# The first stage of an attention, Fourier and expert kernel cut into finer steps and put into a new order

## The chip, the cores and the metric

The kernel runs on one core of a Trainium2 chip. The metric is the device time of one execution in microseconds (us). Five engines work side by side, each on its own queue and in its queue's order: PE (matrix products), DVE (vector), ACT (scalar functions and copies), POOL (a second elementwise engine) and SP, which here only issues DMAs. An engine waits for another by a semaphore.

## What is computed

```python
def reference(**kwargs):
    attn_out = _attn_ref(q, k, v, mem_k, mem_v)        # 4 x 8 heads, 768 rows, chunks of 32 rows with 56 + 8 keys
    x = attn_out.transpose(0, 2, 1, 3).reshape(B, S, H * D)
    x = _moe_ref(x, w_ch1, w_ch2)                      # u = x + real(fft2(x)); u + relu(norm(u) @ w_ch1) @ w_ch2
    return _moe2_ref(x, w_in, conv_w, w_out)           # h = relu(x @ w_in); h * sigmoid(conv3(h)) @ w_out
```

Four batches of 768 rows and 512 columns; the inner widths are 2048 and 1024. The dense weights come as 64-bit floats and are taken apart on the chip ("decoded") into a high and a low part.

## The kernel before

**First stage.** Attention is done in 32 units of 96 rows. For one unit: scores (8 products `sc`, written to a pair of PSUM tiles of which there is only one pair), row maxima of each head (`sm`, `ngm` on DVE), exponentials (ACT, in place in `sm`), transposes in two halves (`atp` on PE, copied to `at`), the product with the values (`o`), the division (`r`, `xn` on DVE), sums and differences of mirrored columns (`xf` on POOL) and a second transpose (`xtp`, copied to `xT`). After seven or eight units of a batch its Fourier transform can begin (function `dft`: folds, products `z`, products `p`, centring `pm`, then `uc`, the result). After that comes `dense(b)`, the first quarter of the hidden width for both halves of the batch: four blocks `h` with copies `hh` (ACT) and `hl` (DVE), four blocks `y`, each copied out. All of these products share four rotating PSUM banks, later (from the third part on, pool `ps_g2`) three.

**Decoding.** One weight block of 128x512 passes through seven DVE and ACT operations (lines 124 to 140), spread over four steps `W`; 24 blocks are decoded up to the main loop and in its first turns.

**The order.** A string, `SCHED`, line 38, says in which order steps are recorded; `task` (line 549) plays a letter: S scores and row maxima, E exponentials of half a unit, A transposes of half a unit and their copy, P values product and division, X second transpose and its copy, B one step of the transform, D one step of `dense`, W one step of decoding, F one filler product (`keep`, line 204), H one step of the split of the first chunk of the main loop. Every engine's queue gets its instructions in this order. `ENGINES` says which engine does which copy or sum. A bar in the string divides it into three parts: with the attention, the rest of the transforms, the rest of `dense`. Then follows the main loop (lines 748 to 786): for a chunk and block f a product group `h` (12 products), and two turns later four groups `acc`, which read `hh` and `hl`. The main loop and the last layer after it are PE-bound and take two thirds of the time.

Of the kernel before, what the change touches and what calls it, by code (L numbers as in the profile page):

```python
# [37 lines left out]
SCHED = "FFFSEAEFSAWFWFFFEEPFFFSFFAFFWWAEPAFXSWFEAWESFFEWWPSFFEFFWXXAAEWWPEAFFSEFFFWAPAFFFEAXFEPAAFFFSFFFFFFWEFEXWPAASWXEWEPAXFFSFFBAPEEAXASFEBPSFAEBBFEFFFWBASEBXPXABASFEBWEBPAESFAWBBXBEPAAEESFBBBWBWXPASFBEABBWWBBBBXPEASFWXEAFFBWWPBEBEWASEBBAXEWPXAAFBSFEBBWEPSABBAWBWEXEDDWDWDPSAABEXDPDBBEBBBDABDAXESBBPDBEEBBXBABSDXBABPSEBBADBBABDPABDEBSEAXBBEBBEEPBSBABXBADBDEBBPEXABASDPBDADBDBBSXEXBDABESBPEABEABDBBSPBADFBBFEBXAEESDBBBBPABABBXDEPDBBAAEBXEBBBXBDBPADABDBPXDDXBB|BBBWDWBDWBBDWBDDDBBWWWBBWDDWBBBBWDWBWWDBDBWBWBWWWBWDWBWDDWWBWBBBWBBDBDBWDDBWBB|DDWDDWWDWWWWWDDWWWDWWHDWHDHDWHDWWWDDDWDWWWWWWW"  # L38
ENGINES = {'at': 'aaaaaaaaavavaaaaaaaaaaaaaaaaaaaaaaaaaaaaaaaaaavaaaavaaavaaaaaaaa', 'xt': 'vvvvaaaaaaaaaaaaavaaaaaaaaavaava', 'y': 'aaaaaaaaaaaaaaaaaaaaaaaaaaaaaaaa', 'uh': 'aaaaaaaaaaavavvvvaaavvaaavavaaaaaaaaaaavvv', 'ul': 'vvpvvvvvvvvvvvvpvvvvvvvvvpvvpppppvpvvvpppv', 'fl': 'pvvvvppvppvvppvp', 'f': 'vpvvvpppvpvpvvpv', 'u0': 'vvvvvvvv', 'u1': 'vvvvvvvv'}
# [7 lines left out]
def fourier_mixer_kernel(ctx: ExitStack, tc: tile.TileContext, qk, vw, w1, w2, w_in, w_out, conv_w,  # L47
# [57 lines left out]
    def decode_all(todo, st=None):  # L105

        st, lo_of = st or fetch(todo[0][0]), None
        for i, (_, where, f, spill) in enumerate(todo):
# [3 lines left out]
            while placed(f) is False:  # L112
                if lo_of is not None:
                    lo_of()
                    lo_of = None
                yield
# [51 lines left out]
    def run(gen, n=1):  # L168
        for _ in range(n):
            if next(gen, "end") == "end":  # L170
                return False
        return True
# [30 lines left out]

    def keep(n):

        p = ps_g.tile([128, 512], F32, tag="g", name="idle")
        for _ in range(n):
            mm(p[:, 0:128], onesm, onesm, start=True, stop=True)  # L208

    NUNITS = NB * NU  # L210
    units = {}
    def load_qk(u):
        if u < NUNITS:
            t = ldp.tile([128, QW + KWD], F32, tag="qk", name="qk", bufs=2)
            units[u] = {"qk": t}
            nc.sync.dma_start(out=t, in_=qk[u])

    def load_v(u):
        if u < NUNITS:
            t = ldp.tile([128, VW], F32, tag="vw", name="vw", bufs=3)  # L220
            nc.sync.dma_start(out=t, in_=vw[u])
            units[u]["vw"] = t

    def scores(u):
# [3 lines left out]
        kT = t[:, QW:QW + KWD].rearrange("p (a k) -> p a k", a=4)  # L228
        sc = [ps_sc.tile([128, 4, KW], F32, tag="sc", name="sc") for _ in range(2)]
        sch = {}  # L230
        for a in range(4):
            for g in range(2):
                sch[2 * a + g] = sc[g][:QB, a, :]
                mm(sch[2 * a + g], qT[64 * g:64 * g + 64, a, :], kT[64 * g:64 * g + 64, a, :], start=True, stop=True)  # L234
        blk = u % NU
        kind = 0 if blk == 0 else (2 if blk == NU - 1 else 1)
        sm = smp.tile([QB, NH, KW], F32, tag="sm", name="sm", bufs=3)
        ngm = smp.tile([QB, NH], F32, tag="ngm", name="ngm")
# [4 lines left out]
        d["ex"], d["ngm"] = sm, ngm  # L243
# [7 lines left out]
    def atr(u, half):  # L251
        d = units[u]
        if half == 0:
            d["at"] = smp.tile([128, NH, QB], F32, tag="at", name="at", bufs=1)
        at = ps_g.tile([128, 4, QB], F32, tag="g", name="atp")
        for i in range(4):
            nc.tensor.transpose(at[:, i, :], d["ex"][:, 4 * half + i, :], ident_sb[:QB, :QB])  # L257
        copy("at", d["at"][:, 4 * half:4 * half + 4, :], at)

    def pv(u):  # L260
# [3 lines left out]
        r = smp.tile([QB, NH], F32, tag="r", name="r")  # L264
        o = ps_o.tile([128, 2, 512], F32, tag="o", name="o")
        oh = o[:QB, :, 0:VW // 2].rearrange("p b (h e) -> p b h e", e=HD + 1)
        for h in range(NH):
            mm(oh[:, h // 4, h % 4, :], at_sb[:, h, :], vw[:, h * (HD + 1):(h + 1) * (HD + 1)], start=True, stop=True)  # L268
        r4 = r.rearrange("p (b h o) -> p b h o", b=2, o=1)
        nc.vector.tensor_scalar(out=r4, in0=oh[:, :, :, HD:HD + 1], scalar1=1e-9, scalar2=None, op0=ALU.add)  # L270
        nc.vector.reciprocal(out=r, in_=r)
        xn = smp.tile([QB, DM + 1], F32, tag="xn", name="xn", bufs=1)
        nc.vector.tensor_tensor(
            out=xn[:, 0:DM].rearrange("p (b h e) -> p b h e", b=2, e=HD), in0=oh[:, :, :, 0:HD],
            in1=r4.to_broadcast([QB, 2, 4, HD]), op=ALU.mult)
        xf = smp.tile([QB, 2, 256], F32, tag="xf", name="xf")
# [5 lines left out]
    xTs = {}  # L282

    def xtr(u):
        d = units.pop(u)
        b, blk = divmod(u, NU)
        if blk == 0:
            xTs[b] = xtp.tile([128, 4, S + 1], F32, tag="xT", name="xT")
        xT = xTs[b]
        xf = d["xf"].rearrange("p a (m c) -> p (a m) c", c=128)  # L290
        p = ps_g.tile([128, 4, QB], F32, tag="g", name="xtp")
        for i in range(4):
            nc.tensor.transpose(p[:, i, :], xf[:, i, :], ident_sb[:QB, :QB])  # L293
# [10 lines left out]
    def dft(b):  # L304
# [3 lines left out]
        for sl, rv in ((slice(97, 385), slice(671, 383, -1)), (slice(0, 97), slice(768, 671, -1))):  # L308
# [3 lines left out]
            while NU * b + NU - 1 in units or count["X"] < NU * b + NU:  # L312
# [21 lines left out]
        def zstep(c, m):  # L334
# [5 lines left out]
            z = ps_g.tile([128, 512], F32, tag="g", name="z")  # L340
# [9 lines left out]
            accumulate(z[:sn, 0:nw], seq)  # L350
            zh = dfp.tile([97, 256], F32R, tag=f"zh{c % 2}{m}", name="zh")
# [6 lines left out]
            if c < 2:  # L358
                nc.vector.tensor_tensor(out=zn[:sn, 1], in0=z[:sn, 256:258], in1=zn[:sn, 0].bitcast(F32),
                                        op=ALU.subtract)  # L360
                ZN[c, m] = zn
            Z[c, m] = (zh, zl, sn)
# [21 lines left out]
        zstep(0, 0)  # L384
        yield from fold(2)
        yield
        zstep(0, 1)
        yield from fold(3)
        yield
        zstep(1, 0)  # L390
        yield
        zstep(1, 1)
# [4 lines left out]
        for m in range(2):  # L397
            zc = slice(128 * m, 128 * m + 128)
            p = ps_g.tile([128, 512], F32, tag="g", name="p")
            accumulate(p[:, 0:194], part(0, 194, zc))  # L400
            accumulate(p[:, 256:448], part(1, 192, zc))
            pj = p.rearrange("p (r j) -> p j r", r=2)
# [16 lines left out]
        def center(hf, gs):  # L419
            ss = slice(hf * HALF, hf * HALF + HALF)  # L420
            pm = ps_g.tile([128, 512], F32, tag="g", name="pm")
            mm(pm[:, 0:HALF], onesm, gs, start=True, stop=True)  # L422
            for m in range(2):
                nc.vector.tensor_tensor(out=G[:, m, ss], in0=G[:, m, ss], in1=pm[:, 0:HALF], op=ALU.subtract)
            nc.scalar.copy(gs[0:1, :], pm[0:1, 0:HALF])
            nc.sync.dma_start(out=mud[b][:, ss], in_=gs[0:1, :])

        gs = summed(0)
        for c in (2, 3):
            for m in range(2):  # L430
                zstep(c, m)
                yield
            center(c - 2, gs)
# [3 lines left out]
        for m in range(2):  # L437
            zc = slice(128 * m, 128 * m + 128)
            p = ps_g.tile([128, 512], F32, tag="g", name="p")
            for c, o, n in ((2, 0, 194), (3, 256, 192)):  # L440
# [4 lines left out]
                accumulate(p[:, o:o + n], seq[-1:], start=False)  # L445
            pj = p.rearrange("p (r j) -> p j r", r=2)
# [11 lines left out]
            yield  # L458
        uc = dfp.tile([128, 4, S], F32, tag="Fhl", name="uc")
        for hf in range(2):  # L460
# [5 lines left out]
            yield  # L466
            yield from split_uc(2 * b + hf, uc[:, :, ss])
            if hf:
                bgb.append(dense(b))
# [14 lines left out]
    def g1(c, f):  # L484
        uh, ul = uhl[c]
        need(("1", f))
        p = ps_g.tile([128, 512], F32, tag="g", name="h")
        accumulate(p[:, 0:TC], split3([(w1h[f][:, k * 128:k * 128 + 128], w1l[f][:, k * 128:k * 128 + 128],
                                        uh[:, k], ul[:, k]) for k in range(4)]))
        hh = a1p.tile([128, TC], F32R, tag="hh", name="hh", bufs=NI)  # L490
# [3 lines left out]
                                       op0=ALU.max, op1=ALU.subtract)  # L494
        hhl[c, f] = (hh, hl)

    def dense(b):
        for hf in range(2):
            c = 2 * b + hf
            for f in range(NI):  # L500
                g1(c, f)
                yield
            for t in range(4):
                ts = slice(t * 128, t * 128 + 128)
                need(*[("2", f) for f in range(NI)])
                p = ps_g.tile([128, 512], F32, tag="g", name="y")
                accumulate(p[:, 0:TC], split3([(w2h[f][:, ts], w2l[f][:, ts]) + hhl[c, f] for f in range(NI)]))
                y = a1p.tile([128, TC], F32, tag="y", name="y")
                copy("y", y, p[:, 0:TC])
                nc.sync.dma_start(out=yd[b][:, t, hf * TC:hf * TC + TC], in_=y)  # L510
# [23 lines left out]
    bga, bgb = [], []  # L534

    def step_of(q):
        moved = False
        while q:
            got = next(q[0], "end")
            if got != "end":  # L540
                return moved or got != "wait"
            q.pop(0)
            moved = True
        return moved

    count = dict.fromkeys("SEAPXW", 0)
    todo = {}

    def task(k):
# [5 lines left out]
        if k == "S":  # L555
            scores(n)
            load_qk(n + 2)
            if n == 0:
                load_v(2)
        elif k == "E":  # L560
            expo(n // 2, n % 2)
            if n == 8:
# [3 lines left out]
                nc.gpsimd.dma_start(out=stab_sb, in_=stab)  # L566
        elif k == "A":
            atr(n // 2, n % 2)
        elif k == "P":
            pv(n)  # L570
            load_v(n + 3)
        elif k == "X":
            xtr(n)
            if n % NU == NU - 2:
                bga.append(dft(n // NU))
        elif k == "F":
            keep(1)
        elif k == "B":
            return step_of(bga)
        elif k == "D":  # L580
            return step_of(bgb)
# [4 lines left out]
    with tc.manual_schedule():  # L586
        load_qk(0)
        nc.scalar.dma_start(out=mask_sb, in_=mask)
        load_qk(1)
# [4 lines left out]
        wdec = decode_all([({"1": w1, "2": w2}[k][f], place, (k, f), None) for k in "12" for f in range(NI)],  # L594
# [438 lines left out]
```

## Time and profile before

| | |
|---|---|
| runs | 1018.87 and 1019.71 us, median of three 1019.71 |
| profiled execution, its own time | 1020.89 us |
| its span, first to last instruction | 1018.1 us |
| busy in the span | PE 98%, DVE 67%, ACT 43%, POOL 21% |
| filler products | 63 (126 instructions), all but two of them before 114 us |
| first block `h` | 117.78 us |
| last four groups `y` of `dense` begin | 334.07 us |
| first product of `acc`, the main loop's | 348.63 us |

A busy PE is a PE with an instruction in flight. The first stage is the only long stretch in which PE is less than full and the other engines are close to full; from 150 us on PE has no gap until 740 us.

### The profile page before, as it was taken

What the parts mean: (1) busy time and instruction counts of PE and PEld (TensorE: products, weight loads), DVE (VectorE), ACT (ScalarE), POOL (GpSimd) and SP (SyncE); (2) the same over time, 40 slices, a digit from 0 to 9 for tenths busy, and PEclk for the clock granted to TensorE, in tenths of its full rate; (3) what the DMA queues carried; (4) which work ended last, traced back from release to release, by engine and by line L of the source; (5) the groups of instructions that cost most, each with busy time, mean ns of one, the idle gap of its engine ahead of it and who ended that gap; (6) DMA issues with size and microseconds to landing.
All of it is one profiled execution on the core that took longest, in us unless ns stands there. A gap on an engine that the chain in (4) does not pass through costs nothing.

```text
span 1018.1 us, 16674 instructions
## 1 busy us (share of the span) xinstructions
PE 999.1 (98%) x6430; PEld 957.6 (94%) x6430; DVE 685.8 (67%) x1508; ACT 442.5 (43%) x923; POOL 214.9 (21%) x232
## 2 busy tenths in 40 slices
PE   7899999999999999999999999999999999999997
PEld 6888989999999999999999999999999999999996
DVE  4889956766988775767787775635357566465554
ACT  4687754664444423333333332212245454454442
POOL 1353251422400000102211000202013222222222
PEclk9999999999999999999999999999999999999999
DMA  6864532522437545575788972818543111010101
GB/s 198 264 185 138 182 105 78 164 72 81 129 100 235 179 152 194 187 182 125 174 201 224 199 183 83 148 49 164 159 123 115 52 69 56 1 62 1 62 1 62
DMA packets 63807, 130.86 MB, mean 129 GB/s; under 512 B 4919, under 2 KB 39199, under 8 KB 63503
## 3 DMA queue, kind: packets, MB, share of 16 engines
q1 hardware_dynamic: 51424, 102.35, 30.6%
q0 software_dynamic: 12048, 27.17, 14.9%
q8 instruction: 50, 0.82, 0.3%
q14 instruction: 29, 0.24, 0.1%
q10 hardware_dynamic: 256, 0.28, 0.1%
HBM read 92.28 MB, written 43.79 MB: 134 GB/s over the span
## 4 chain that ended last, share of the span: by engine, by line
PE 90%; DVE 5%; issue 2%; ACT 1%; DMA 1%; POOL 1%; DVEq 0%; POOLq 0%; ACTq 0%
PE acc L66 32%; PE h L66 25%; PE ph L66 12%; PE y L66 6%; PE o L268 3%; PE sc L234 2%; PE p L66 2%; PE z L66 2%; DVE sm L240 2%; PE atp L257 2%; PE idle L208 1%; PE xtp L293 1%; PE pm L422 1%; ACT sm L248 0%; DMA qk<-in_qk 0%
## 5 line engine op out<-in xcount | busy, mean ns | idle before, releaser
L66 PE MATMUL acc<-hh,w 128*128 128x384 f32 x768 | 208.0, 334 | 0.0
L66 PE MATMUL h<-uh,w 128*128 128x384 f32 x768 | 208.0, 334 | 0.0
L492 ACT ACTIVATE hh<-h 128x384 fp32r<-128x384 f32 x128 | 62.5, 490 | 247.2 <-PE h L66 247.1
L493 DVE SCALAR_TENSOR_TENSOR hl<-h,hh 128x384 fp32r<-128x384 f32 x128 | 70.5, 554 | 145.6 <-ACT hh L492 145.1
L66 PEld LDWEIGHTS acc<-hh,w 128*128 128x128 f32 x768 | 139.8, 188 | 0.0
L66 PEld LDWEIGHTS h<-uh,w 128*128 128x128 f32 x768 | 139.8, 188 | 0.0
L66 PE MATMUL ph<-xh,wit 128*128 128x384 f32 x512 | 136.3, 337 | 0.7 <-ACT hrow L823 0.7
L66 PE MATMUL acc<-hl,w 128*128 128x384 f32 x384 | 128.3, 334 | 0.0
L66 PE MATMUL h<-ul,w 128*128 128x384 f32 x384 | 128.3, 334 | 0.0
L66 PE MATMUL acc<-wot,hgh 128*128 128x512 f32 x384 | 119.6, 393 | 0.0
L831 DVE SCALAR_TENSOR_TENSOR cv<-hrow,cw_sb,cv 128x768 f32<-128x768 f32 x64 | 110.1, 1721 | 3.1 <-ACT cv L825 2.0
L843 POOL TENSOR_TENSOR hgl<-cv,hgh 128x768 fp32r<-128x768 f32 x32 | 60.4, 1886 | 194.6 <-ACT hgh L842 179.0
L837 DVE TENSOR_TENSOR cv<-hrow,cv 128x768 f32<-128x768 f32 x32 | 30.7, 959 | 99.2 <-ACT cv L836 99.1
L66 PEld LDWEIGHTS ph<-xh,wit 128*128 128x128 f32 x512 | 93.3, 188 | 2.6 <-ACT hrow L823 1.4
L66 PE MATMUL ph<-xl,wit 128*128 128x384 f32 x256 | 86.1, 336 | 0.0
L66 PEld LDWEIGHTS acc<-wot,hgh 128*128 128x128 f32 x384 | 71.7, 188 | 13.4
L248 ACT ACTIVATE sm<-sm,ngm 96x128 f32<-96x128 f32 x256 | 80.5, 394 | 7.4 <-DVE ngm L240 7.4
L823 ACT ACTIVATE hrow<-ph 128x384 f32<-128x384 f32 x64 | 31.3, 493 | 102.3 <-PE ph L66 101.1
L66 PE MATMUL acc<-wot,hgl 128*128 128x512 f32 x192 | 74.7, 389 | 0.0
L66 PEld LDWEIGHTS acc<-hl,w 128*128 128x128 f32 x384 | 72.1, 188 | 0.0
L66 PEld LDWEIGHTS h<-ul,w 128*128 128x128 f32 x384 | 72.1, 188 | 0.0
L240 DVE CUSTOM_DVE_ANT_0 sm<-sc,mask_sb 96x128 f32<-96x128 f32 x256 | 56.3, 282 | 18.3 <-PE sc L234 14.5
(150 smaller groups left out, 1879.2 us busy)
## 6 DMA issues: line engine op xcount, KB each, us to landing
w<-in_w SPq DMA_DIRECT2D x32, 512.0 KB, 4.1
qk<-in_qk SPq DMA_DIRECT2D x32, 448.0 KB, 3.5
us<-ucd SPq DMA_DIRECT2D x13, 768.0 KB, 7.9
yp<-yd SPq DMA_DIRECT2D x13, 768.0 KB, 8.4
vw<-in_vw SPq DMA_DIRECT2D x32, 260.0 KB, 3.0
ucd<-uc SPq DMA_DIRECT2D x8, 768.0 KB, 4.7
yd<-y SPq DMA_DIRECT2D x32, 192.0 KB, 2.0
ucd<-mud POOLq DMA_DIRECT2D x8, 768.0 KB, 14.4
```

What stands on the lines that cost most here:

```text
L66: mm(o, a, b, start=(start and i == 0), stop=(stop and i == n - 1))
L234: mm(sch[2 * a + g], qT[64 * g:64 * g + 64, a, :], kT[64 * g:64 * g + 64, a, :], start=True, stop=True)
L240: nc.vector.tensor_tensor_reduce(out=sm[:, h, :], in0=sch[h], in1=mask_sb[:, kind, :], op0=ALU.add, op1=ALU.min, scale=-0.125, scalar=3e38 ...
L248: nc.scalar.activation(out=d["ex"][:, h, :], in_=d["ex"][:, h, :], func=AF.Exp, scale=-1.0, bias=d["ngm"][:, h:h + 1])
L257: nc.tensor.transpose(at[:, i, :], d["ex"][:, 4 * half + i, :], ident_sb[:QB, :QB])
L268: mm(oh[:, h // 4, h % 4, :], at_sb[:, h, :], vw[:, h * (HD + 1):(h + 1) * (HD + 1)], start=True, stop=True)
L492: nc.scalar.activation(out=hh, in_=p[:, 0:TC], func=AF.Relu)
L493: nc.vector.scalar_tensor_tensor(out=hl, in0=p[:, 0:TC], scalar=0.0, in1=hh.bitcast(F32), op0=ALU.max, op1=ALU.subtract)
L823: nc.scalar.activation(out=h[:, 1 + hf * TC:1 + hf * TC + TC], in_=p[:, 0:TC], func=AF.Relu)
L831: nc.vector.scalar_tensor_tensor(out=cv, in0=h[:, j:j + S], scalar=cw_sb[:, j, f:f + 1], in1=cv, op0=ALU.mult, op1=ALU.add)
L837: nc.vector.tensor_tensor(out=cv, in0=h[:, 1:S + 1], in1=cv, op=ALU.mult)
L843: nc.gpsimd.tensor_tensor(out=hgl[i], in0=cv, in1=hgh[i].bitcast(F32), op=ALU.subtract)
```

## The change

Steps are cut finer. S keeps the products alone, and T does the row maxima of half a unit; A and X keep the transposes, and a and x do the copies; P is cut into P (product), p (add), r (reciprocal) and n (multiply and the POOL sums); l and v issue the loads of a unit; B and D yield between a product group and the copies that read it. Assertions check that no step is recorded before the last reader of its buffer. The core of the diff:

```diff
@@ scores
-        for h in range(NH):
+    def rowmax(u, half):
...
+        for h in range(4 * half, 4 * half + 4):
             nc.vector.tensor_tensor_reduce(
@@ atr
         for i in range(4):
             nc.tensor.transpose(at[:, i, :], d["ex"][:, 4 * half + i, :], ident_sb[:QB, :QB])
-        copy("at", d["at"][:, 4 * half:4 * half + 4, :], at)
+
+    def atr_out(u, half):
...
+        copy("at", d["at"][:, 4 * half:4 * half + 4, :], at[:, 0:4 * QB].rearrange("p (a q) -> p a q", a=4))
@@ dense
-                g1(c, f)
+                p = g1(c, f)
...
+                yield "half"
+                g1_out(c, f, p)
                 yield
...
                 accumulate(p[:, 0:TC], split3([(w2h[f][:, ts], w2l[f][:, ts]) + hhl[c, f] for f in range(NI)]))
+                yield "half"
                 y = a1p.tile([128, TC], F32, tag="y", name="y")
                 copy("y", y, p[:, 0:TC])
@@ prelude
-        load_v(0)
-        load_v(1)
-        nc.sync.dma_start(out=sgn_sb, in_=sgn)
...
+                nc.gpsimd.dma_start(out=sgn_sb, in_=sgn)
```

The string and the table of engines are new. The string has 5 letters F where 63 stood. The numbers of products of the other kinds are unchanged, and so are the counts of `sc`, `atp`, `o` and `xtp` that stand ahead of the first `z`. Of the copies of `y`, all on ACT before, 18 of 32 go to DVE now; of the 16 sums `uc`, all on DVE before, 5 go to POOL. The letters W are 33, 27 and 26 in the three parts before, 34, 17 and 36 now. The third parts of the two strings (before, change; a D was a whole step before and is half of one now):

```
DDWDDWWDWWWWWDDWWWDWWHDWHDHDWHDWWWDDDWDWWWWWWW
DDDDDDWWWDDDWDDWDDDWWWDHDWWDWWWDHWWWWWWWWDDWWWWWDWDWWWWWWWWW
```

**PE, the start of the program.** Before (`idle` is the filler):

```order
L208 MATMUL idle<-onesm 128x128 x3
L234 MATMUL sc<-qk 96x128 x8
L257 MATMUL atp<-ident_sb,sm 128x96 x4
L208 MATMUL idle<-onesm 128x128
L234 MATMUL sc<-qk 96x128 x8
L257 MATMUL atp<-ident_sb,sm 128x96 x4
L208 MATMUL idle<-onesm 128x128 x4
L268 MATMUL o<-vw,at 96x65 x8
L208 MATMUL idle<-onesm 128x128 x3
L234 MATMUL sc<-qk 96x128 x8
```

Of the change:

```order
L270 MATMUL sc<-qk 96x128 x8
L227 MATMUL idle<-onesm 128x128
L304 MATMUL atp<-ident_sb,sm 128x96 x4
L270 MATMUL sc<-qk 96x128 x8
L304 MATMUL atp<-ident_sb,sm 128x96 x4
L320 MATMUL o<-vw,at 96x65 x8
L270 MATMUL sc<-qk 96x128 x8
L304 MATMUL atp<-ident_sb,sm 128x96 x8
L270 MATMUL sc<-qk 96x128 x8
```

The products stand in much the same order; the fillers between them are gone.

**DVE, from the end of `dense` to the main loop.** In both programs DVE has four `hl` of the last chunk of `dense`, then decoding, then three `hl` of the main loop in a row, which its first `acc` reads. Before, the last of the four and the rows that follow it (17 rows stand between it and the three `hl`; `whb`, one for a weight block, stands among them three times):

```order
L493 SCALAR_TENSOR_TENSOR hl<-h,hh 128x384
L132 SCALAR_TENSOR_TENSOR whb<-w_4624,wsc 128x512
L136 TENSOR_SCALAR wsc<-whb 128x512
L140 SCALAR_TENSOR_TENSOR w_9_4463<-wlb,wsc 128x512
L124 TENSOR_SCALAR wsc<-w_4673 128x512
L125 TENSOR_SCALAR wlb<-w_4673 128x512
L129 SCALAR_TENSOR_TENSOR wlb<-w_4673,wlb 128x512
L132 SCALAR_TENSOR_TENSOR whb<-w_4673,wsc 128x512
L136 TENSOR_SCALAR wsc<-whb 128x512
L140 SCALAR_TENSOR_TENSOR w_9_4464<-wlb,wsc 128x512
```

Of the change, the same `hl` (here the second of a pair) and what follows; 52 rows stand between it and the three `hl`, with `whb` eight times, three copies of `y` and the split `uh`, `ul` of the first chunk:

```order
L582 SCALAR_TENSOR_TENSOR hl<-h,hh 128x384 x2
L137 SCALAR_TENSOR_TENSOR whb<-w_4359,wsc 128x512
L141 TENSOR_SCALAR wsc<-whb 128x512
L145 SCALAR_TENSOR_TENSOR w_6_3736<-wlb,wsc 128x512
L129 TENSOR_SCALAR wsc<-w_4502 128x512
L130 TENSOR_SCALAR wlb<-w_4502 128x512
L166 COPY y<-y 128x384
L134 SCALAR_TENSOR_TENSOR wlb<-w_4502,wlb 128x512
L137 SCALAR_TENSOR_TENSOR whb<-w_4502,wsc 128x512
L141 TENSOR_SCALAR wsc<-whb 128x512
L145 SCALAR_TENSOR_TENSOR w_7_3737<-wlb,wsc 128x512
```

The decoder stands at block 6 there, where it stood at block 9 before; at the three `hl` of the main loop it stands at block 10 in both.

## Rows read from the trace of the kernel before

**Rows 1.** Stretches: length, then busy us (instructions) by engine, PEclk, DMA share, GB/s.

```profile
0.00:117.78 117.78, 106.27 (x1082) 96.02 (x1083) 93.75 (x463) 82.24 (x238) 39.23 (x70) 1.00 0.63 194
80.00:100.00 20.00, 19.04 (x198) 17.76 (x197) 18.36 (x85) 13.73 (x44) 6.64 (x13) 1.00 0.41 125
100.00:117.78 17.78, 17.33 (x188) 16.01 (x189) 17.30 (x74) 15.30 (x43) 4.61 (x8) 1.00 0.57 178
117.78:180.26 62.48, 60.92 (x512) 58.48 (x510) 42.85 (x168) 34.91 (x101) 23.24 (x31) 1.00 0.32 104
180.26:334.07 153.81, 153.81 (x1129) 150.06 (x1129) 123.09 (x312) 76.32 (x185) 40.25 (x49) 1.00 0.40 130
```

**Rows 2.** Timeline of PE, first stage: start, us, what, count [idle before, releaser].

```profile
5.05 2.02 PE L234 MATMUL sc<-qk 64*96 64x128 f32 x16 [2.31 <-DMA qk<-in_qk]
9.60 2.03 PE L234 MATMUL sc<-qk 64*96 64x128 f32 x16
13.76 1.50 PE L268 MATMUL o<-vw,at 128*96 128x65 f32 x16
15.91 1.12 PE L234 MATMUL sc<-qk 64*96 64x128 f32 x16
...
25.50 1.32 PE L234 MATMUL sc<-qk 64*96 64x128 f32 x16 [1.01 <-DVE ngm L240]
...
47.73 1.83 PE L208 MATMUL idle<-onesm 128*128 128x128 f32 x14
49.40 0.49 PE L293 MATMUL xtp<-ident_sb,xf 96*128 96x96 f32 x4
```

**Rows 3.** Timeline of DVE, the first row maximum of the kernel.

```profile
7.10 0.29 DVE L240 CUSTOM_DVE_ANT_0 sm<-sc,mask_sb 96x128 f32<-96x128 f32 x1 [6.05 <-PE sc L234]
```

**Rows 4.** Chain of work that ended last, 100 to 131 us: start, us, what.

```profile
99.90 0.42 PE idle L208 x2
...
110.83 1.74 DVE uc L166 x2
...
123.35 2.43 DVE wlb L129
...
130.10 2.35 PE y L66 x12
```

**Rows 5.** Groups by line, 0 to 300 us: busy us, mean ns | idle before.

```profile
L161 DVE COPY at<-atp 128x384 f32<-128x384 f32 x5 | 2.7, 548 | 0.2 <-PE atp L257 0.2
L166 POOL TENSOR_TENSOR Fhl<-F,Fhl 128x386 fp32r<-128x386 f32 x4 | 4.4, 1100 | 11.8 <-ACT Fhl L325 11.8
```

**Rows 6.** Timeline of PE, end of dense to main loop.

```profile
334.07 0.33 PE L66 MATMUL y<-hh,rxc 128*128 128x384 f32 x1
...
348.63 0.34 PE L66 MATMUL acc<-hh,w 128*128 128x384 f32 x1
348.81 0.34 PE L66 MATMUL acc<-hl,w 128*128 128x384 f32 x1
```

**Rows 7.** Timeline of DVE, the same place.

```profile
321.94 0.69 DVE L140 SCALAR_TENSOR_TENSOR w<-wlb,wsc 128x512 fp32r<-128x512 int32 x1
...
325.25 0.69 DVE L140 SCALAR_TENSOR_TENSOR w<-wlb,wsc 128x512 fp32r<-128x512 int32 x1
...
331.01 1.82 DVE L166 TENSOR_TENSOR ul<-us,uh 128x768 fp32r<-128x768 f32 x2
...
334.80 0.56 DVE L493 SCALAR_TENSOR_TENSOR hl<-h,hh 128x384 fp32r<-128x384 f32 x1 [0.43 <-ACT hh L492]
335.27 0.68 DVE L132 SCALAR_TENSOR_TENSOR whb<-w,wsc 128x512 int32<-128x512 int32 x1
...
341.71 0.69 DVE L132 SCALAR_TENSOR_TENSOR whb<-w,wsc 128x512 int32<-128x512 int32 x1 [3.04 <-ACT wsc L128]
...
347.37 0.43 DVE L124 TENSOR_SCALAR wsc<-w 128x512 int32<-128x512 int32 x1 [0.47 <-DMA w<-in_w]
...
348.05 1.01 DVE L493 SCALAR_TENSOR_TENSOR hl<-h,hh 128x384 fp32r<-128x384 f32 x2
```

More of the change, by code (lines that the diff above doesn't have):

```diff
@@ L166, in either, with run @@
         (nc.vector if vector(what) else nc.gpsimd).tensor_tensor(out=out, in0=in0, in1=in1, op=op)
[L168 to L172, printed above, removed]
+    def run(gen):
+        return next(gen, "end") not in ("end", "wait")
     def rxt(tag, name):
@@ L202, in fourier_mixer_kernel, with bank, taken, after @@
     sgn_sb = cst.tile([128, 1], F32, name="sgn_sb")
+    banks = []
+    def bank(name):
+        i = len(banks) - PSG
+        assert i < 0 or banks[i][1], "the bank's last product is still unread"
+        t = ps_g.tile([128, 512], F32, tag="g", name=name)
+        banks.append([t, False])
+        return t
+    def taken(*tiles):
+        for entry in banks[-PSG:]:
+            entry[1] |= any(entry[0] is t for t in tiles)
+    def after(k, n):
+        assert count[k] >= n, "a step comes before the last reader of its buffer"
     def keep(n):
-        p = ps_g.tile([128, 512], F32, tag="g", name="idle")
+        p = bank("idle")
+        taken(p)
         for _ in range(n):
@@ L211, in fourier_mixer_kernel, with home @@
     units = {}
[L212 to L222 removed]
+    loop = [u for u in range(NUNITS) if u not in AHEAD]
+    def home(u):
+        d = units.setdefault(u, {})
+        if u in AHEAD and "home" not in d:
+            d["home"] = a1p.tile([128, 4 * TC], F32R, tag=AHEAD[u], name="qv").bitcast(F32)
+        return d
+    def load_qk(u):
+        d = home(u)
+        if u in AHEAD:
+            d["qk"] = d["home"][:, 0:QW + KWD]
+        else:
+            if loop.index(u) > 1:
+                after("S", loop[loop.index(u) - 2] + 1)
+            d["qk"] = ldp.tile([128, QW + KWD], F32, tag="qk", name="qk", bufs=2)
+        nc.sync.dma_start(out=d["qk"], in_=qk[u])
+    def load_v(u):
+        d = home(u)
+        if u in AHEAD:
+            d["vw"] = d["home"][:, QW + KWD:QW + KWD + VW]
+        else:
+            if loop.index(u) > 2:
+                after("P", loop[loop.index(u) - 3] + 1)
+            d["vw"] = ldp.tile([128, VW], F32, tag="vw", name="vw", bufs=3)
+        nc.sync.dma_start(out=d["vw"], in_=vw[u])
     def scores(u):
@@ L282, in fourier_mixer_kernel, with xtr_out @@
     xTs = {}
+    spent, spent_u = set(), set()
     def xtr(u):
-        d = units.pop(u)
+        d = units[u]
+        xf = d["xf"].rearrange("p a (m c) -> p (a m) c", c=128)
+        p = d["xtp"] = bank("xtp")
+        p = p[:, 0:4 * QB].rearrange("p (a q) -> p a q", a=4)
+        for i in range(4):
+            nc.tensor.transpose(p[:, i, :], xf[:, i, :], ident_sb[:QB, :QB])
+    def xtr_out(u):
+        xp = units.pop(u)["xtp"]
+        p = xp[:, 0:4 * QB].rearrange("p (a q) -> p a q", a=4)
+        taken(xp)
         b, blk = divmod(u, NU)
         if blk == 0:
+            assert b < 2 or b - 2 in spent, "the rows before last are still read"
             xTs[b] = xtp.tile([128, 4, S + 1], F32, tag="xT", name="xT")
         xT = xTs[b]
[L290 to L293, printed above, removed]
         xo = xT[:, :, blk * QB:(blk + 1) * QB]
@@ L466, in dft @@
             yield
+            assert b == 0 or 2 * b + hf - 2 in spent_u, "the chunk before last is still read"
             yield from split_uc(2 * b + hf, uc[:, :, ss])
             if hf:
-                bgb.append(dense(b))
+                split_done.add(b)
             yield
@@ L533, in fourier_mixer_kernel, with all_dft, all_dense @@
     wit = []
[L534 to L546, printed above, removed]
+    def all_dft():
+        for b in range(NB):
+            while count["x"] < NU * b + NU - 1:
+                yield "wait"
+            yield from dft(b)
+    def all_dense():
+        for b in range(NB):
+            while b not in split_done:
+                yield "wait"
+            yield from dense(b)
+    split_done = set()
+    count = dict.fromkeys("lvSTEAaPprnXxWBDH", 0)
     todo = {}
@@ L630, in fourier_mixer_kernel @@
         ps_g.release()
+        assert all(entry[1] for entry in banks)
+        banks.clear()
         ps_g = tc.alloc_tile_pool(name="ps_g2", bufs=3, space=PSUM, reuse_waits="tile")
```

138 lines of the change are left out of this document (95 added, 43 removed).

## The prediction

> **What bounds the kernel now.** I read the table of stretches first, then PE's own timeline in the first stage, then the chain of work that ended last, and at last the timelines of DVE and PE where `dense` hands over to the main loop. From 180 us on PE is busy without a gap [rows 1], so whatever is won ahead is kept only if PE is fed through the end of `dense` as it is now. The first stage is another matter. Up to the first `h` at 117.78 us PE shows 106.27 us of work, DVE 93.75 and ACT 82.24 [rows 1]. That PE figure is swollen by fillers: 14 instructions, which are 7 fillers, take from 47.73 to 49.40 us, 1.67 us, so one costs 0.24 us [rows 2]; the 61 that stand ahead of the first `h` make 14.6 us. The work that counts on PE is therefore some 91.7 us, less than DVE's. PE also waits for DVE, as for the 1.01 us before the scores at 25.50 [rows 2]. DVE cannot begin on row maxima before 7.10 us [rows 3]; from there to 117.78 it has 110.7 us and fills some 93.5 of them, 84%. Late in the stage it fills more: 18.36 of 20 us (92%) and 17.30 of 17.78 (97%) [rows 1], and the chain there goes mostly through DVE, with few pieces of filler [rows 4]. So the first stage is bound by DVE and by waits among three engines, not by the fillers.
>
> **The change, part by part.**
>
> *Fillers.* 58 go, 58 x 0.24 = 13.9 us of PE. That is no gain by itself where the next product waits for DVE; it is room for PE.
>
> *Finer steps.* They remove no product and add no operation. They let DVE and ACT do other work between a product and its copy. How full DVE then gets sets the first `h`. Its work ahead of that point also shrinks by 6.7 us: counted over the rows ahead of the first `h` in both orders, four `uc` sums are gone (1.74 for two, so 3.5 us [rows 4]; two go to POOL, two stand later), three `xT` copies and one `at` copy go to ACT (4 x 0.5 = 2.0 us by the 548 ns of such a copy [rows 5], less overlap) and two subtractions `Fhl` go to POOL (about 1.2 us together on DVE; 1.1 us each on POOL [rows 5]). POOL has the room, 39.23 of 117.78 us busy [rows 1]; with no cover its slower sums would put some 2 to 3 us on the way to the first `h`. That leaves 93.5 - 6.7 = 86.8 us. With DVE full all the time the first `h` would come at 93.9; PE, 91.7 us of work from 5.05 on [rows 2], cannot be there before 96.8; at 92% of DVE it is 7.1 + 86.8/0.92 = 101.4; at today's 84% it is 110.4. With three engines this evenly loaded none of them stays full, so I take 105, a gain of 12.8 us with bounds of 7 and 21. After that PE has 1.56 us of gaps up to 180.26 [rows 1] and two fillers, 0.5 us, to lose; I count 0.2 of it, since DVE is still on the chain until 130.10 [rows 4]. Gain in all: **13 us**.
>
> *Loads as steps of their own.* The SP queue starts as before with two `qk` and the identity; the first weight block goes ahead of the first values, which were wanted at 13.76 us only [rows 2]. The DMA share of the first stage, 0.63 [rows 1], rises to 0.63 x 117.78/105 = 0.71; I cost it at nothing, the cover being the two units of lead that the `qk` buffers give; without it a late `qk` costs what the first one did, 2.31 us [rows 2]. The move of `sgn_sb` to POOL costs nothing: it is read only at the end of a transform.
>
> *The decode steps moved into the third part.* Here the order of DVE decides. PE's sequence at this place is the same in both programs: four `h`, four `y`, three `h` of the main loop, then `acc`, whose second product reads `hl`. Before, `y` begins at 334.07 and that second product runs at 348.81 [rows 6], 14.7 us later. DVE ended its last `hl` of `dense` at 335.27, when `whb` begins, and began the three `hl` of the loop at 348.05 [rows 7]: 12.8 us, of which 3.04 and 0.47 were waits. It was just in time, 0.76 us ahead less the 0.5 us that one `hl` takes. In the change the same stretch of DVE holds 52 rows instead of 17, with eight `whb` instead of three. One weight block takes 325.25 - 321.94 = 3.31 us of DVE [rows 7]. From the first `whb` to the eighth are 7 periods, 23.2 us; the rest of the eighth block and the first two operations of the next one, which stand ahead of `hl`, are 3.31 less the 0.6 us of the third operation, 2.7; three copies of `y` at the cost of a DVE copy of that size, 548 ns less some 0.08 that it overlaps with the next [rows 5], 1.4; the split of the first chunk, one half `ul` of 0.91 [rows 7] and one `uh` of about 0.5, 1.4. Sum 28.7 us. On the old clock the first `hl` would start at 335.27 + 28.7 = 364.0 and end at 364.5; PE wanted it at 348.81. **PE stalls 15.7 us** in the sum. Nothing on DVE can overtake, since a queue runs in order, and PE has nothing else in its queue. Part of the stall is taken earlier: `h` of the loop and `y` share three PSUM banks, and two copies of `y` stand behind four to six blocks of decoding, on ACT and on DVE, so the second and third `h` wait for a bank. That moves the stall, it does not add to it. Bounds: 13 us if the copies and the split fit into waits; 22 us if each of the seven blocks waits 0.47 us for its weights as at 347.37 [rows 7] and one operation takes 2.43 us as `wlb` at 123.35 did [rows 4]. The decoding was done ahead of it, in the second part (27 W, now 17), under PE work: DVE is busy there 123.09 of 153.81 us [rows 1], so it cost nothing, and now DVE has free time there that nothing fills.
>
> *PE's clock.* The first two scores take 2.02 us at 5.05 and 9.60, the third 1.12 at 15.91 [rows 2], with 16 instructions each: after the idle start PE ran at its lower level, 1.2 GHz, until about 13 us, and at 2.4 GHz from there on, fillers or not, through gaps of 1 us; the granted clock in every stretch reads 1.00 [rows 1]. In the stall PE would be idle two or three times for some 3 to 7 us each, which the trace of before shows nowhere after the start. The bound below is nothing, the bound above is what the start cost: between 5.05 and 13 us, 8 us of products at half speed, 4 us lost. I take **2 us**. The Trainium skill, page "TensorE: Matmul & The Clock Gate", section "HAM oscillation — how this bites in real kernels", says that waits between bursts of products let the gate throttle PE again and that the next burst starts at half rate, over and over. By that rule the stall costs its clock loss on top, and thinner work in the first stage without fillers could do the same there; its second half is a rival below. The row at 25.50 after a gap agrees only that a gap of 1 us does not do it.
>
> *Sum.* 1018.1 - 13 + 15.7 + 2 = 1022.8 us of span. The median of the runs lies 1.6 us above that span (1019.71); so 1024 us.
>
> **The rivals.**
>
> A. *The stall is hidden.* It would need DVE to reach its three `hl` 15 us earlier than the sum, by decoding faster than 3.31 us a block or by PE being late. The row at 341.71 shows DVE waiting for ACT there, so the old stretch had slack, but slack in waits doesn't shorten seven periods. Time: 1019.71 - 13 = 1006.7.
>
> B. *The first stage gives nothing.* DVE stays at 84% or new waits take the fillers' place (one pair of score tiles: scores, maxima and scores again follow each other strictly). Against it: 61 fillers and DVE at 92 to 97% later. Time: 1019.71 + 17.7 = 1037.4.
>
> C. *PE falls to its lower level in the first stage.* The fillers kept PE busy; without them it has 91.7 us of work in 105. For it: the start shows that level [rows 2]. Against it: the gaps are near 1 us, and at half speed PE would at once be fuller. Each us of work at the lower level costs a us more, of which 13 us are hidden by PE's own room (105 less 91.7). From 30 us of such work on, the kernel is slower by more than 2%: 1024 + 30 - 13 = 1041; if half the stage's work is hit, 1024 + 46 - 13 = 1057. The rule of the Trainium skill named above speaks for this case, and no row before shows it after 13 us.
>
> **How the numbers follow.** The forecast 0.75, A 0.11, B 0.09, C 0.05. Within the forecast the gain may be 7 to 18 and the stall with its clock 13 to 24, so 1015 to 1032 holds most of it, and 1025 +- 11 leaves out A, the worse end of B and C. Range 1010 to 1034. About 2% is what a measurement of this kernel can tell from no change, 999.3 and 1040.1: faster needs A and a gain above 20 us, 0.03; slower is C and B with the worst stall, 0.07; the same 0.90.
>
> **What would show it.** First `h` near 105 us with DVE over 88% busy up to there; five fillers; PE without a gap above 1.5 us until then. At the first `acc`: DVE with 25 us or more of decoding between `hl` of `dense` and of the loop, PE idle 14 us or more in sum between the second `y` and that `acc`, released by ACT `y`, DVE `y` and DVE `hl`. From `acc` to the end the same length as before, 669.5 us. The prediction is wrong if PE has no gap there, or if the scores take 2 us each later than 20 us.

## The result, and the profile after the change

| | before | after |
|---|---|---|
| median | 1019.12 us (7 runs: six of 1018.53 to 1019.74, one stray of 2529.63) | 1028.73 us (7 runs, 1024.51 to 1031.25) |
| ratio to before | | 1.0089, 95% interval 1.0066 to 1.0112 |
| span of the profiled execution | 1018.1 us | 1026.9 us (its own time 1028.73) |
| first block `h` | 117.78 us | 109.58 us |
| from there to the last four `y` of `dense` | 216.29 us | 215.22 us |
| from the first of these `y` to the second product of `acc` | 14.74 us | 31.92 us |
| from there to the end | 669.3 us | 670.2 us |

The kernel is 0.9% slower. The four stretches close the account of the two profiled executions: 8.2 and 1.1 us are won up to the end of `dense`, 17.2 and 0.9 are lost behind it, and 8.8 us is the difference of the spans. In each stretch PE runs the same products in both columns, but for the fillers, so the loss lies at the place that the prediction names, and the gain in the first stage is smaller than it says.

The stretches of after, in the columns of [rows 1]: the first stage, two pieces of it, and the end of `dense`.

```profile
0.00:109.58 109.58, 93.72 (x967) 85.43 (x967) 85.61 (x453) 82.36 (x238) 48.58 (x75) 0.94 0.64 202
...
20.00:40.00 20.00, 13.39 (x154) 12.02 (x154) 14.12 (x84) 14.21 (x42) 9.75 (x18) 0.92 0.98 282
40.00:60.00 20.00, 19.06 (x180) 17.77 (x180) 12.70 (x67) 13.23 (x40) 8.03 (x11) 0.73 0.47 157
...
324.80:356.72 31.92, 18.27 (x86) 16.20 (x85) 30.07 (x55) 13.38 (x22) 1.87 (x1) 0.86 0.48 152
```

The first row answers to the first of [rows 1]: DVE has 85.61 us of work ahead of the first `h` where it had 93.75. New are the second and third row: in 20 to 40 us PE has 13.39 us of work only while the DMA share stands at 0.98, and in 40 to 60 us its granted clock is 0.73, where every stretch before read 1.00. (At the start of the program that column reads 1.00 too, before and after, although 16 scores take 2.02 us there [rows 2]; so at the start the level is read off the length of the products.) In the last row DVE is nearly full (30.07 of 31.92) and PE is not (18.27).

PE at the end of `dense`, its timeline with idle time and releaser in brackets, answering to [rows 6]:

```profile
324.80 0.33 PE L67 MATMUL y<-hh,rxc 128*128 128x384 f32 x1
...
335.36 0.41 PE L67 MATMUL h<-uh,w 128*128 128x384 f32 x1 [2.04 <-DVE y L166]
...
343.41 0.69 PE L67 MATMUL h<-uh,w 128*128 128x384 f32 x1 [5.54 <-ACT y L168]
...
348.20 0.44 PE L67 MATMUL h<-uh,w 128*128 128x384 f32 x1 [0.58 <-DVE y L166]
...
355.31 0.69 PE L67 MATMUL acc<-hh,w 128*128 128x384 f32 x1 [4.76 <-ACT hh L581]
356.72 0.69 PE L67 MATMUL acc<-hl,w 128*128 128x384 f32 x1 [0.72 <-DVE hl L582]
```

Where before had no gap at all there are five, 13.64 us in sum. Behind the two longest of them products take 0.69 us at first, where they take 0.33 without a gap. The releasers named are the copies of `y`, which free the banks, then `hh` and `hl`; all of them stand behind decoding, as DVE at the same place shows (answering to [rows 7]):

```profile
325.58 0.56 DVE L582 SCALAR_TENSOR_TENSOR hl<-h,hh 128x384 fp32r<-128x384 f32 x1 [1.52 <-ACT hh L581]
326.06 0.68 DVE L137 SCALAR_TENSOR_TENSOR whb<-w,wsc 128x512 int32<-128x512 int32 x1
...
339.90 0.68 DVE L137 SCALAR_TENSOR_TENSOR whb<-w,wsc 128x512 int32<-128x512 int32 x1
...
343.21 0.69 DVE L137 SCALAR_TENSOR_TENSOR whb<-w,wsc 128x512 int32<-128x512 int32 x1
...
356.12 1.48 DVE L582 SCALAR_TENSOR_TENSOR hl<-h,hh 128x384 fp32r<-128x384 f32 x3
```

The eight `whb` are there, 3.31 us from one to the next in the quiet part, and 30.1 us lie from the first of them to the three `hl` of the main loop, where it was 12.8 before.

PE in the first stage of after, in the columns of [rows 2]:

```profile
14.01 1.12 PE L270 MATMUL sc<-qk 64*96 64x128 f32 x16
...
33.27 0.50 PE L304 MATMUL atp<-ident_sb,sm 96*128 96x96 f32 x4
40.61 2.03 PE L270 MATMUL sc<-qk 64*96 64x128 f32 x16 [6.84 <-DMA qk<-in_qk]
...
46.54 2.03 PE L270 MATMUL sc<-qk 64*96 64x128 f32 x16
...
55.52 1.12 PE L270 MATMUL sc<-qk 64*96 64x128 f32 x16
```

PE waits 6.84 us for the load of the ninth unit. Behind the wait the scores of two units take 2.03 us, as at the start of the program, and the next ones, at 55.52, take 1.12 again; from 40.61 to 50.70 us the granted clock is 0.50. So PE loses time twice, once in the wait and once through the clock. What was in the DMA queues then, by issues (name, count, KB each, median us from issue to landing), of 27 to 42 us:

```profile
stab_sb<-in_stab POOLq DMA_DIRECT2D x1, 1176.1 KB, 12.1
dtab_sb<-in_dtab POOLq DMA_DIRECT2D x1, 1028.0 KB, 6.4
```

The two tables of the transform, 2.2 MB, were issued at 27.84 and 29.59 us, and the load that PE waited for at 29.05. It was issued 4.7 us before PE stood for it (33.77), and the scores came 11.6 us after the issue; the loads of `qk` in that stage whose landing the trace has take 3.3 to 5.1 us. Before, the two tables were issued at 33.31 and 35.30 us, and PE waited for a `qk` at the start only.

### The profile page after: what moved, and what is told of

Its sections match the earlier page's. It is cut to its first block, busy times and chain, and to the rows that moved or that the text cites. A ratio compares the mean times of both kernels' runs of the same rounds, so it can differ in the third digit from the quotient of the medians.

```text
span 1026.9 us, 16453 instructions
## 1 busy us (share of the span) xinstructions
PE 992.0 (97%) x6314; PEld 949.2 (92%) x6314; DVE 680.0 (66%) x1527; ACT 432.0 (42%) x895; POOL 235.3 (23%) x242
## 3 DMA queue, kind: packets, MB, share of 16 engines
q1 hardware_dynamic: 51280, 102.35, 30.1%
## 4 chain that ended last, share of the span: by engine, by line
PE 91%; DVE 5%; DMA 2%; ACT 1%; issue 1%; POOL 0%; ACTq 0%; DVEq 0%; POOLq 0%
PE acc L67 32%; PE h L67 25%; PE ph L67 12%; PE y L67 6%; PE o L320 4%; PE sc L270 3%; PE p L67 3%; PE z L67 2%; PE atp L304 2%; DMA qk<-in_qk 2%; PE xtp L359 1%; DVE w L145 1%; PE pm L502 1%; ACT sm L292 0%; DVE wlb L130 0%
## 5 line engine op out<-in xcount | busy, mean ns | idle before, releaser
L67 PE MATMUL h<-uh,w 128*128 128x384 f32 x768 | 210.4, 337 | 8.2 <-ACT y L168 5.5
```

The source lines that it names most:

```text
L67: mm(o, a, b, start=(start and i == 0), stop=(stop and i == n - 1))
```

## Experiments

### The decode steps moved back

Three places of the order string: 13 of the letters W of the third part spread over the second, and the third part from the last `dense` chunk on as in the kernel before (with its four letters H where the change has two). In words:

```diff
-17 W in the second part, 36 in the third (31 of them behind the last h of dense)
+30 W in the second part (13 more, evenly spread), 23 in the third:
+"WWWWWDDDDWWWDDWWHDDWHDDHDDWHDDWWWDDDDDDWDDWWWWWWW"
```

> The changed kernel with 13 of its decode steps moved from the third part into the second, so that 30 steps are done before the last eight blocks of `dense`, as in the kernel before; the rest of the change stays. If the place of the decode steps makes the stall: no gap of PE above 1 us between the second y of the last chunk and the first acc (13.6 us in sum in the changed kernel), granted clock 1.00 there, and 1028.7 - 17.2 = 1011.5 us (1008 to 1014). If the y copies on DVE and the three banks make it wherever the decoding stands: gaps above 8 us remain, 1020 or more. If the 13 steps cost the second part what they save in the third: 1015 to 1020, with gaps of PE between 180 and 307 us.

Measured: 1016.54 us (10 runs, 1011.18 to 1025.78), ratio 0.9965 (0.9931 to 0.9998). In the profiled execution (1018.42 us) the stall is gone: between 325 us and the first `acc` PE has one gap above 1 us, and the granted clock is 1.00 from 53 us to the end:

```profile
25.25 2.02 PE L270 MATMUL sc<-qk 64*96 64x128 f32 x16
...
332.64 0.44 PE L67 MATMUL y<-hh,rxc 128*128 128x384 f32 x1 [1.49 <-DVE hl L582]
```

The time is 12 us below the changed kernel and not 17; it lies in the range of the third case of the expectation, not of the first. Two losses are seen. The evenly spread steps stand ahead of copies of the transform and cost PE gaps in the second part: 2.4 us without work in 180 to 307 us, 0.1 in after (1.63 us for `zn` at 275.91 the longest). And the first stage of that execution was slower than that of after: 16 scores still took 2.02 us at 25.25, and the first `h` came at 112.12. The runs also spread over 14 us, where 25 runs of before beside them spread over 5.3 (1018.66 to 1024.00). What makes the spread is looked at further down. The place of the decode steps made the stall.

### The decode steps alone moved in the kernel before

The opposite edit, with nothing else of the change (two of the four letters H of the third part go from the string with it, as in the change). In words:

```diff
-27 W in the second part, 26 in the third (11 behind the last h of dense)
+17 W in the second part, 36 in the third: "DDDDD" and
+"DDDWWWDWDWDDWWWHDWWWWWDHWWWWWWWWDWWWWWWDWWWWWWWWW"
```

> The kernel before with nothing but its decode steps moved: 10 from the second part into the third, and in the third to where the changed kernel has them (31 behind the last h of dense instead of 11). If that alone makes the stall: DVE takes 26 to 28 us from the last hl of dense to the hl of the loop (12.8 before), PE is idle 12 to 14 us in sum there, the granted clock falls, and the time is 1019.1 + 16 = 1035 us (1031 to 1038). If the copies of y on DVE or the finer steps are needed for the stall: below 1025.

Measured: 1037.09 us (4 runs), ratio 1.0160 (1.0127 to 1.0192), 17.3 us more than before. What PE waited for from 330 to 370 us (in total, times, longest):

```profile
PE h L66 <- ACT y L163: 6.1, 2, 5.4
PE acc L66 <- ACT hh L492: 4.9, 1, 4.9
PE acc L66 <- DVE hl L493: 0.7, 1, 0.7
PE h L66 <- DVE ul L166: 0.4, 1, 0.4
```

That is 12.1 us, and the granted clock falls twice, to 0.84 over 333 to 365 us. From the first `whb` (335.10) to the three `hl` (363.60) DVE takes 28.5 us. That is 15.7 us more than before, and the time is 17.3 us longer. All copies of `y` are on ACT here, so the three on DVE are not needed for the stall. The order of the third part alone, decoding above all, brings what the change loses at this place.

### The tables later

```diff
             if n == 8:
                 nc.gpsimd.dma_start(out=dtab_sb, in_=dtab)
 ...
+            if n == 16:
                 nc.gpsimd.dma_start(out=stab_sb, in_=stab)
                 nc.gpsimd.dma_start(out=sgn_sb, in_=sgn)
```

> The changed kernel with the second of the two large tables of the transform (stab, 1176 KB, and sgn) issued four units later, at the 17th half unit of exponentials instead of the 9th. If the 6.84 us in which PE waits for qk at 33.8 us comes from the tables taking the DMA engines: that wait falls below 2 us, the granted clock stays 1.00 up to 60 us, the first h comes at 101 to 104 us instead of 109.55, and the time is about 1022 (1019 to 1025). If the loads are late because they are issued late (the buffers of qk come free two units before): the wait stays near 7 us and the time above 1027. If the load only collides later: first h near 109, a wait for qk or vw above 4 us somewhere up to 80 us.

Measured: 1025.97 us (10 runs), ratio 1.0067 (1.0037 to 1.0096). By time alone it can't be told from the changed kernel, since the intervals overlap, and the time lies above the 1019 to 1025 that were expected. Its profiled execution, the fastest of the ten (1022.57 us), shows the mechanism:

```profile
37.63 2.02 PE L270 MATMUL sc<-qk 64*96 64x128 f32 x16 [2.45 <-DMA qk<-in_qk]
...
42.41 1.17 PE L270 MATMUL sc<-qk 64*96 64x128 f32 x16
```

The wait for the same load is 2.45 us instead of 6.84 (below 2 was expected), the clock falls all the same but is back after one unit instead of two, and the first `h` comes at 103.58. So the load was late at least in part because it shared the DMA engines with `stab`. Whether the rest of the wait comes from the other table, `dtab`, was not tried.

### Fillers in the wait

```diff
+        if u == 8:
+            for _ in range(25):
+                mm(sc[0][:, 0, :], onesm, onesm, start=True, stop=True)
```

> The changed kernel with 25 more filler products ahead of the scores of the ninth unit (6 us at 0.24 us each), where PE waits 6.84 us for qk. The wait for the load is not shortened by them; they only keep PE at work. If the fall of the granted clock (0.73 in 40 to 60 us) costs time of its own: clock 1.00 there, first h near 105.5 us instead of 109.55, 1024.7 us (1023 to 1026). If the other engines or the loads set the pace there: clock 1.00, first h within 1 us of 109.55, 1028 to 1029.

Measured: 1023.35 us (10 runs, 1021.68 to 1035.06), ratio 1.0041 (1.0010 to 1.0071), 5.4 us below the changed kernel in the median. The two intervals still touch; six of the ten runs lie below the fastest of the changed kernel. The granted clock holds behind the wait:

```profile
39.41 5.77 PE L268 MATMUL sc<-onesm 128*128 128x128 f32 x50
46.44 1.12 PE L273 MATMUL sc<-qk 64*96 64x128 f32 x16 [1.25 <-DMA qk<-in_qk]
```

The scores come 7.0 us after PE has come to this place, as in the changed kernel, and take 1.12 us instead of 2.03. The median fits a fall of the clock that has a price of its own, near what was expected. The profiled execution, one of the slowest (1030.58 us), can't show that price: its first `h` comes at 111.13, since, as in the first experiment, PE came late to its upper level. Ahead of the wait 16 scores took this long:

```profile
25.10 2.02 PE L273 MATMUL sc<-qk 64*96 64x128 f32 x16
29.84 1.12 PE L273 MATMUL sc<-qk 64*96 64x128 f32 x16
```

The instructions up to there are those of the changed kernel, whose execution had 1.12 at 14.01 us. PE was at work nearly all the time in both. When PE reaches its upper level (2.4 GHz; the lower is 1.2) is therefore not fixed without the old fillers: in the four executions shown so far (after, tables_late, w_early, fill_wait) 16 scores first took less than 1.4 us at 14.01, 18.35, 29.70 and 29.84 us.

### The kernel before without its fillers

```diff
-63 letters F in the string
+none
```

> The kernel before without its 63 fillers, nothing else moved. If the fillers take PE time that is wanted: up to 13.9 us less, 1005 to 1012. If DVE sets the pace and PE's clock does not care: within 2 us of 1019.5. If the fillers are what brings PE to its upper level by 13.5 us and keeps it there (the changed kernel came there at 13 us in one profiled execution and at 17 to 29 us in others): products still take 2.0 us for 16 scores after 16 us, the executions spread by 5 us or more, and the time is 1022 to 1030.

Measured: 1024.27 us (10 runs, 1019.19 to 1028.67), ratio 1.0034 (1.0011 to 1.0056). Taking 15 us of fillers away makes the kernel 4.7 us slower in the median. In its profiled execution (1027.22 us):

```profile
0.00:125.03 125.03, 107.28 (x961) 95.05 (x961) 93.64 (x463) 82.76 (x238) 39.21 (x70) 0.86 0.58 182
```

PE shows 107.28 us of work, as much as with the fillers [rows 1], because the same products run longer: the granted clock falls five times up to 105 us and reads 0.86 as a mean. DVE has the same 93.6 us, and the first `h` comes at 125.03. PE came to its upper level early here, without fillers (16 scores take 1.12 us at 13.57); what it did not do is stay there. The fillers of the kernel before were its clock's upkeep.

### Fillers at the start

The first of the experiments, w_early, with fillers ahead of the first three scores:

```diff
+        for _ in range({0: 7, 1: 2, 2: 6}.get(u, 0)):
+            mm(sc[0][:, 0, :], onesm, onesm, start=True, stop=True)
```

> The kernel w_early with 15 fillers more at the start: 7 ahead of the first scores, where PE waits 5 us for its first load, 2 ahead of the second and 6 ahead of the third. If the spread of w_early (1011 to 1026) comes from the time at which PE reaches its upper level: 16 scores take 1.1 us by 15 us, the first h comes by 109.6 us, the spread shrinks below 5 us, median 1011 to 1013. If the spread has another source (the loads): median 1015 to 1018 and the same spread.

Measured: 1014.40 us (5 runs, 1013.53 to 1016.40), ratio 0.9942 (0.9919 to 0.9964). The spread falls from 14 us (ten runs) to 3 (five), as expected if the start of the clock made it; the median falls by 2 us, less than hoped. 16 scores take 1.12 us at 5.11, 2.02 at 9.18 and 1.12 again at 14.79. What is left is the wait for the ninth unit, 6.27 us, and the clock behind it; this kernel still issues the tables early.

### All of it together, and the division of the copies

best1 has the decode steps early (behind steps of `dense` only), the last eight copies of `y` on ACT, `stab` late, the 15 fillers at the start and 8 ahead of the ninth scores. best1_old_engines is best1 with the division of copies, splits, folds and sums of the kernel before. Its edit in words:

```diff
-ENGINES of the change ('at' 17 on DVE, 'ul' 17, 'u0' 4 and 'u1' 1 on POOL, ...)
+ENGINES of before ('at' 5 on DVE, 'ul' 12 on POOL, 'u0' and 'u1' all on DVE, ...)
```

> The changed kernel with the decode steps early as in w_early (but behind steps of `dense` alone), the last eight copies of y on ACT as before, stab issued late, 15 fillers at the start as in w_early_warm and 8 ahead of the ninth scores. If the losses named so far are all of them: no gap of PE above 1 us from 60 us to 740, granted clock 1.00, first h at 100 to 104 us, 1003 us (1000 to 1008). If the loads only collide elsewhere: a wait for qk or vw above 4 us, first h at 107 or later, 1009 to 1013.

> The kernel best1 with the kernel before's division of the first stage's copies, splits, folds and sums among ACT, DVE and POOL (only the copies of y stay). It puts some 6.7 us of work back on DVE ahead of the first h. If DVE sets the first h: 3 to 6 us later than in best1, and the time as much longer. If PE or the loads set it: within 1 us of best1.

Measured: best1 1010.05 us (4 runs, 1006.09 to 1012.85), ratio 0.9890 (0.9850 to 0.9929); best1_old_engines 1016.06 us (10 runs, 1012.86 to 1018.00), ratio 0.9958 (0.9943 to 0.9972). The first stage of each, up to its own first `h`, best1 first:

```profile
0.00:102.22 102.22, 96.52 (x1012) 87.94 (x1013) 85.42 (x453) 82.30 (x238) 48.57 (x75) 1.00 0.66 217
```

```profile
0.00:110.69 110.69, 100.85 (x1012) 91.14 (x1013) 91.60 (x466) 83.20 (x239) 43.26 (x71) 0.94 0.64 208
```

In the profiled execution of best1 (1007.38 us) PE waits no more at the ninth unit, where it has its eight fillers; the clock does not fall any more once 16 scores take 1.12 us (15.82), and the first `h` comes at 102.22, inside what the prediction bounds by 96.8 and 110.4. From 7.29, its first row maximum, DVE fills 85.2 of 94.9 us, 90%. The median of best1 lies above the 1000 to 1008 of its first case: two of its four runs take 1006.09 and 1007.38 us at a mean granted clock of 1.000, the two others 1012.71 and 1012.85 at 0.994. With 6.2 us of work put back on DVE the first `h` is 8.5 us later and the median 6.0. So the division of the work sets it, through DVE. How much of this is DVE's queue itself is open: the clock fell three times in that execution, twice just behind a wait of PE for row maxima (1.72 us at 67.84, 1.39 at 103.09), and the order of the steps, which stayed, was made for the new division. best1 keeps three gaps behind 300 us, 1.42 us for a copy of `y`, 1.62 and 1.03 for `hl`.

### The last gaps, and more fillers

best2 has 33 decode steps in the second part and 20 in the third, none right ahead of the last `hl`, and only the last four copies of `y` moved to ACT. best2_hold adds two fillers ahead of the scores of nine more units.

```diff
+third part: "DDWWDDWDDWWDDWWHDDWHDDHDDWHWWDDDDWWDDWDDWWWWWW"
+best2_hold: fillers {0: 7, 1: 2, 2: 6, 3: 2, 4: 2, 5: 2, 6: 2, 7: 2, 8: 8, 9: 2, 10: 2, 11: 2, 12: 2}
```

> The kernel best1 with three decode steps more in the second part (33 and 20) and the steps in the third part put so that none stands right ahead of the hl of the last chunk; of the copies of y only the last four on ACT. If the three gaps of PE that best1 shows behind 300 us (1.4, 1.6 and 1.0 us, 4.0 in sum) come from where these steps stand: gaps below 1.5 us in sum, 1006 to 1007 us against 1010. If they come with the number of steps: the gaps move, 1009 to 1011.

> The kernel best2 with 18 fillers more, two ahead of the scores of each of units 3 to 7 and 9 to 12 (18 x 0.24 = 4.3 us of PE). If the spread of best1 (1006 to 1013) comes from falls of PE's granted clock in the first stage: clock 1.00 there, spread below 3 us, median 2 to 4 us below best2. If the loads make the spread, or the fillers stand in the way of products: the same spread, median the same or up to 4 us above best2.

Measured: best2 1006.97 us (4 runs, 1004.45 to 1007.16), ratio 0.9849 (0.9810 to 0.9887), the fastest of all. From 300 to 375 us PE has 0.9 us of gaps in all, and in 300 to 340 us PE works 39.11 of 40. best2_hold 1010.58 us (5 runs, 1010.05 to 1016.22), ratio 0.9905 (0.9872 to 0.9938), with this in its profiled execution, the slowest (1016.22 us):

```profile
57.74 2.02 PE L272 MATMUL sc<-qk 64*96 64x128 f32 x16 [2.36 <-DMA qk<-in_qk]
```

Here a wait of 2.36 us for a load at another unit went with a fall of the clock for 10 us, and the first `h` came at 112.52: more fillers don't rule such a fall out. The other four runs, at a mean granted clock of 0.998 to 1.000, take 1010.05 to 1011.18 us, some 3.5 us more than best2, near the 4.3 us that the 18 fillers take. So where the clock holds, they stand in the way of products. In best1 and here the slow runs are those with the lower clock; what lets it fall in one execution and not in another is open. Why the loads of this variant come late at that unit was not tried.

## Why the prediction came out as it did

**The end of `dense`: right in place and cause; its total is right in part by luck.** The sum put 28.7 us from the first `whb` to the three `hl`; it was 30.1. The delay of the second `acc` product was to be 15.7 us and the clock's loss 2 on top; measured are 31.92 - 14.74 = 17.2 us of delay and 0.9 behind it, 18.1 in all against 17.7. So the delay was 1.5 us too small, since DVE took longer, and the clock's loss 1.1 too large, and the two misses nearly cancel. The granted clock did fall, with each of the two gaps near 5 us, and products inside the stall took up to twice as long. But PE waited there for DVE, which went from one row to the next without a wait from 326.06 us on: slower products only turned waiting into work (13.64 us of gaps where 17.2 were lost). That the stall doesn't need copies of `y` on DVE is what the kernel before with late steps shows (12.1 us of gaps with all `y` on ACT). Rival A, a stall that is hidden, is out, and so is B, a first stage that gives nothing.

**DVE's work in the first stage: right.** 86.8 us were worked out from the first row maximum on, 85.4 measured, and best1_old_engines shows that the first `h` moves with this work.

**The first stage's gain: too large by 3.7 us, by two steps that were costed at nothing.** The first `h` came at 109.58, not 105, and DVE was 84% full up to there, not over 88%, with one gap of PE of 6.84 us where none above 1.5 was to be. With 8.2 and 1.1 won, the gain was 9.3 us where 13 stood in the sum. The step that failed first is that of the loads: "I cost it at nothing, the cover being the two units of lead". The lead is of no use when the scores come 11.6 us after the load's issue; with one of the two tables issued later the wait was 2.45 us and the first `h` at 103.58. The text had the rise of the DMA share, 0.71, as a mean of the stage; in the 20 us that mattered it was 0.98. The second is that of the fillers: "room for PE". It was right that taking them away gives nothing by itself, but they were not free to take: the kernel before without them is 4.7 us slower. In the profiled execution of the change PE came to its upper level as early as before, so there their absence shows only in the 10 us behind the load. With the load's wait and the clock repaired (best1) the first `h` came at 102.2, better than the 105 of the sum, so the estimate of what finer steps are worth was sound and even low.

**The signs.** Of the two signs of being wrong that the prediction names, the second came: at 40.61 and 46.54 us, later than 20, the scores took 2.03 us. By its own measure its account of the first stage is wrong, though the time lies in the range.

**Rival C was half true.** It asked for PE at its lower level in 30 us or more of the first stage and was given 0.05; the kernel is not slower by 2%. As a mechanism it came, in smaller pieces: 10 us behind the load and, in two executions of kernels that start with the same instructions (w_early, fill_wait), some 15 us more at the start. It should have stood as a term of a few us in the sum, with the clock's late rise as the upper bound. The rule of the Trainium skill, page "TensorE: Matmul & The Clock Gate", section "HAM oscillation — how this bites in real kernels", that waits between bursts throttle PE again and the next burst starts at half rate, agrees with the 16 scores at 40.61 (2.03 us behind the wait) and with both long gaps in the stall.

**The sum.** 1018.1 - 9.3 + 18.1 = 1026.9 us of span, against 1022.8; of the 4.1 us that the prediction is short, 3.7 are the gain and 0.4 the loss. The range of 1010 to 1034 holds the measured 1028.73 us, and both terms lie inside the bounds that the prediction gave them.

## What to carry to other kernels

Read a reordering on the engine that does the side work: count what stands in its queue between the last row that feeds the old phase and the first that feeds the new one, multiply by the period of the pattern, and hold that against the work that PE has in that time. Side work that is moved from a stretch with free time to one without can cost its full length (DVE's stretch grew by 17.3 us here, the delay was 17.2), and the sum of a gain and a loss hides both: with decoding, tables and fillers put right the kernel is 12.9 us faster than before (best2), and the change as it stands is 9.6 slower. Before products "that do nothing" are taken out, ask which clock the others will run at without them, and when a stage is made faster, look at the DMA load of its worst 20 us, not of the whole stage.

## What the runs showed that was not expected

- PE can be at work for 20 us and stay at 1.2 GHz. With scores, transposes and value products nearly back to back from 5.2 us on, 16 scores took 2.02 us up to 25.25 in one execution (first experiment), and 1.12 from 14.01 on in another with the same instructions up to there (after). With the 63 fillers of before they took 1.12 us by 15.91 [rows 2]. What decides it is open.
- The granted clock fell without a long wait. In the kernel before without fillers the longest gap of PE in 15 to 60 us is 1.62 us, and 16 scores took 1.12 us at 13.57, 1.69 at 21.41, 1.96 at 37.92, 2.03 at 49.27 and 1.12 at 54.68.
- The clock's part of a wait need not be smaller than the wait: 6.84 us of waiting in after were followed by 10 us at a granted clock of 0.50, in which half of PE's time is lost, and so were 2.36 us in best2_hold. Behind the 2.45 us in tables_late the lower clock lasted one unit.
